# Sparse attention and gated MLP on one Trainium2 core: another way into the first batch's attention

## The chip, the cores and the metric

One core of a Trainium2 chip runs the whole program. The metric is device time in microseconds (us) of one execution. TensorE, VectorE, ScalarE, GpSimd and SyncE are written PE, DVE, ACT, POOL and SP, as in the profile. SP issues nearly all DMAs of this kernel, on one queue.

## The reference, cut to what matters

For 4 batches, 8 heads, 768 tokens and head size 64, each query sees the keys less than 16 tokens away and 24 summary keys, one per block of 32 tokens (the maximum over the block; the summary value is the mean). The result, 3072 rows of 512, goes through a gated MLP: `(x @ w_a * (x @ w_b)) @ w_out` with an inner size of 1536. The weights come as 64-bit floats, 18.9 MB, and are turned into pairs of 32-bit words (a high and a low part) on the chip.

```
k_sum = k.reshape(B, H, nb, block, D).max(axis=3)
v_sum = v.reshape(B, H, nb, block, D).mean(axis=3)
scores_l = scale * q @ k.T   where |i - j| < 16, else -1e9
scores_s = scale * q @ k_sum.T + log(32)
a = softmax(concat(scores_l, scores_s));  x = a @ concat(v, v_sum)
out = (x @ w_a) * (x @ w_b) @ w_out
```

## The kernel before, in words

**Tiling.** Query tiles have 128 tokens of all 8 heads. Tiles 0 to 3 (chunks 0 and 1, two tiles each) form the head of the kernel, `first_attention` (line 860); tiles 4 and 5 are chunk 2; the other three batches come in chunks of three tiles. The MLP is cut into 12 slices f of 128 inner columns. An item (`item`, line 1083) is one slice for one chunk: `up` (line 1056, matmuls of line 1067) makes the two products with w_a and w_b, four short steps on ACT and DVE form their product and split it into two parts, and `down` (line 1147, matmuls of line 1154) adds to the output. Slices 0 to 2 and 11 run for chunk 0 and chunk 1 apart, slices 3 to 10 for both together.

**The head's steps.** Keys come as six loads of 128 tokens by 8 heads, one token of one head a packet of 256 B (`first_keys`, lines 485 to 530). PE turns each with four transposes (line 441), DVE takes the block maxima from PSUM (line 508), ACT writes the turned keys to `kT` (lines 500, 501). Queries of a tile come in the same way, are turned (line 441) and scaled by ACT (line 938). For each tile, `scores` (line 638) has PE put the mask into PSUM (line 650) and add the score products (line 663); DVE takes maxima (line 700), ACT the exponentials (lines 721 and 729), DVE the sums and reciprocals, POOL the normalization (line 755). `transposes` (line 761) turns the result (line 768) and ACT copies it (line 780); `values` (line 846, matmuls of line 816) multiplies by the value rows, which come in three loads a tile (`load_values`, line 624, packets of 256 B); ACT and DVE split the result into the x that the MLP reads (lines 835 and 839).

**Value means.** Three loads of 512 KB bring all values, 16 tokens of a head in a partition. Load 0 is summed over its tokens by one DVE reduction (line 899), loads 1 and 2 by four halving additions each on POOL (line 910). 20 small matmuls (line 921) join half blocks, ACT copies the result into the value buffers (line 957, twice) and POOL copies it on to the other tiles' buffers (line 964, six times).

**Weights.** A part (slice f, and a, b or o for the three matrices) is a 512 KB load (line 380), then `convert` (line 386): ACT line 405, DVE lines 408 and 416, ACT line 421 (the high part), POOL line 424 (the low part). A part is called W0a, W0b and so on below.

**Order.** Each operation is put on a list with what it reads and writes. `Work.emit` (line 94) then issues them. The table `ORDER` (line 24) holds, for each engine, the numbers of the operations in the order in which that engine has them for the first part of the program (up to slice 6 or so on PE); after it, a planner with cost estimates chooses. Every engine works strictly in its order. With the numbers resolved, the head before is:

- SP: the six key loads, q0, value load 0, q1, value loads 1 and 2, W0a, q2, W0b, W0o, one value-row load of tile 1, W1a, q3, the three value-row loads of tile 0, the other two of tile 1, W1b, W2a, ...
- PE: keys; turn q0, masks 0, scores 0; turn q1, masks 1, scores 1; transposes and means; turn q2, masks 2, scores 2; values 0; turn q3; values 1; masks 3, scores 3; a transpose of tile 2; then the first up (slice 0 of chunk 0).

Of the kernel before, what the change touches and what calls it, by code (L numbers as in the profile page):

```python
# [29 lines left out]
    ],  # L30
    "ACT": [
# [8 lines left out]
    ],  # L40
    "DVE": [
# [8 lines left out]
    ],  # L50
    "POOL": [
# [3 lines left out]
    ],  # L55
# [88 lines left out]
def attention_moe(  # L144
# [33 lines left out]
    MEANS = "DPP"  # L178
# [61 lines left out]
    pairs = sb([P, 96], "pairs")  # L240
    nc.gpsimd.memset(pairs, 1.0 / BLK)
    for base, sign in ((32, 1), (-31, -1)):
        nc.gpsimd.affine_select(
            out=pairs, in_=pairs, compare_op=ALU.is_ge, fill=0.0, base=base,
            pattern=[[-2 * sign, 96]], channel_multiplier=sign,
        )
# [1031 lines left out]
```

## Time and profile before

| what | us |
|---|---|
| median of 3 runs (lowest to highest) | 654.5 (653.66 to 655.36) |
| span of the profiled execution, first to last instruction | 652.4 |
| PE busy in that span | 639.0 |

The page gives the profiled execution's span; a whole time of that execution is not listed beside it. Between the span and the median lie 2.1 us (1.3 to 3.0 us against the lowest and the highest run). PE's granted clock is 0.997 of full speed on the mean of the span. The span is read in two stretches: the head up to the first item, and the long rest in which PE has one matmul behind the other.

### The profile page before, as it was taken

What the parts mean: (1) busy time and instruction counts of PE and PEld (TensorE: products, weight loads), DVE (VectorE), ACT (ScalarE), POOL (GpSimd) and SP (SyncE); (2) the same over time, 40 slices, a digit from 0 to 9 for tenths busy, and PEclk for the clock granted to TensorE, in tenths of its full rate; (3) what the DMA queues carried; (4) which work ended last, traced back from release to release, by engine and by line L of the source; (5) the groups of instructions that cost most, each with busy time, mean ns of one, the idle gap of its engine ahead of it and who ended that gap; (6) DMA issues with size and microseconds to landing.
All of it is one profiled execution on the core that took longest, in us unless ns stands there. A gap on an engine that the chain in (4) does not pass through costs nothing.

```text
span 652.4 us, 12782 instructions
## 1 busy us (share of the span) xinstructions
PE 639.0 (98%) x4911; PEld 591.7 (91%) x4911; DVE 398.0 (61%) x866; ACT 242.6 (37%) x694; POOL 155.8 (24%) x238
## 2 busy tenths in 40 slices
PE   7799999999999999999999999999999999999997
PEld 4598888899999999999999999999999999999996
DVE  5877899987887584676676763756766632122212
ACT  4886787324443231422334312343323321121111
POOL 6782667523223222123222100111001100000000
PEclk9899999999999999999999999999999999999999
DMA  9999993552422233513114230142110200010001
GB/s 242 277 284 267 296 240 72 102 125 56 104 63 82 50 72 64 128 39 81 33 34 119 54 56 12 26 102 40 32 25 1 72 1 0 2 49 0 1 1 48
DMA packets 153108, 54.68 MB, mean 84 GB/s; under 512 B 133192, under 2 KB 145736, under 8 KB 153048
## 3 DMA queue, kind: packets, MB, share of 16 engines
q1 hardware_dynamic: 152904, 53.75, 34.0%
q8 instruction: 38, 0.62, 0.4%
q14 instruction: 22, 0.18, 0.1%
q10 hardware_dynamic: 144, 0.13, 0.1%
HBM read 47.12 MB, written 6.29 MB: 82 GB/s over the span
## 4 chain that ended last, share of the span: by engine, by line
PE 90%; DMA 4%; SPq 2%; ACT 1%; POOL 1%; DVE 1%; issue 0%; DVEq 0%; POOLq 0%; ACTq 0%
PE h L1067 55%; PE o L1154 28%; DMA raw<-in_moe_w_b_dram 4%; PE c L663 3%; PE o L816 3%; SPq L342 2%; POOL w L424 1%; PE h L816 0%; ACT S L405 0%; DVE c L408 0%; PE c L816 0%; PE c L1067 0%; POOL space L755 0%; DVE S L416 0%; PE o L768 0%
## 5 line engine op out<-in xcount | busy, mean ns | idle before, releaser
L1067 PE MATMUL h<-x,w 128*128 128x384 f32 (+2 forms) x2100 | 390.5, 320 | 0.1
L1067 PEld LDWEIGHTS h<-x,w 128*128 128x128 f32 x2100 | 334.1, 190 | 9.5 <-DVE x L839 0.7
L1154 PE MATMUL o<-w,gh 128*128 128x512 f32 x731 | 175.2, 382 | 0.0
L1154 PEld LDWEIGHTS o<-w,gh 128*128 128x128 f32 x731 | 134.5, 189 | 18.0 <-issue 2.4
L1135 DVE TENSOR_TENSOR h<-h,g 128x384 f32<-128x384 f32 (+1 forms) x79 | 45.7, 579 | 134.7 <-PE h L1067 134.3
L1137 ACT CAST gh<-h 128x384 fp32r<-128x384 f32 x71 | 34.0, 480 | 220.8 <-DVE h L1135 216.4
L800 DVE STREAM_TRANSPOSE pt<-s 32x256 f32<-32x256 f32 x228 | 99.3, 436 | 11.6 <-POOL s L755 7.9
L755 POOL TENSOR_TENSOR s<-s,nml 128x480 f32<-128x480 f32 x44 | 43.5, 989 | 229.6 <-DVE nml L751 193.6
L1067 PE MATMUL h<-late,w 128*128 128x384 f32 x288 | 94.0, 326 | 0.0
L729 ACT ACTIVATE s<-s,nml 128x120 f32<-128x120 f32 x160 | 61.5, 387 | 35.1 <-DVE nml L700 35.1
L1132 ACT COPY g<-h 128x384 f32<-128x384 f32 (+1 forms) x80 | 39.2, 490 | 55.4 <-PE h L1067 54.5
L1067 PEld LDWEIGHTS h<-late,w 128*128 128x128 f32 x288 | 54.4, 189 | 1.2 <-DVE late L839 0.2
L1140 DVE TENSOR_TENSOR gh<-h,gh 128x384 fp32r<-128x384 f32 x71 | 39.5, 556 | 22.0 <-ACT gh L1137 21.3
L692 DVE SCALAR_TENSOR_TENSOR s<-c,mask 128x480 f32<-128x480 f32 x40 | 26.0, 652 | 26.7 <-PE c L663 26.4
L587 POOL TENSOR_TENSOR S<-S 96x256 f32<-96x256 f32 (+3 forms) x58 | 33.2, 572 | 35.4 <-DMA S<-in_v_dram 32.9
L1154 PE MATMUL o<-w,x 128*128 128x512 f32 (+1 forms) x133 | 32.6, 381 | 0.2 <-DVE x L1108 0.2
L424 POOL TENSOR_TENSOR w<-S,w 128x512 fp32r<-128x512 f32 x24 | 30.4, 1286 | 7.3 <-ACT w L421 6.9
L408 DVE TENSOR_SCALAR c<-raw 128x512 int32<-128x512 uint32 x36 | 28.4, 804 | 5.6 <-DMA raw<-in_moe_w_b_dram 3.0
L729 ACT ACTIVATION_READ_ACCUMULATOR s<-s,nml 128x1 f32 x160 | 30.3, 190 | 0.0
L1154 PEld LDWEIGHTS o<-w,x 128*128 128x128 f32 x133 | 24.4, 189 | 4.2 <-DVE x L1108 0.6
L700 DVE TENSOR_REDUCE nml<-s 128x4 f32<-128x480 f32 x40 | 25.8, 647 | 0.5
L405 ACT ACTIVATE S<-raw 128x512 f32<-128x512 f32 x24 | 20.4, 861 | 4.7 <-DMA raw<-in_moe_w_b_dram 4.3
(138 smaller groups left out, 446.3 us busy)
## 6 DMA issues: line engine op xcount, KB each, us to landing
raw<-in_moe_w_a_dram SPq DMA_DIRECT2D x12, 512.0 KB, 7.7
raw<-in_moe_w_b_dram SPq DMA_DIRECT2D x12, 512.0 KB, 8.6
raw<-in_moe_w_out_dram SPq DMA_DIRECT2D x12, 512.0 KB, 5.7
out_dram<-S SPq DMA_DIRECT2D x23, 256.0 KB, 2.1
S<-in_v_dram SPq DMA_DIRECT2D x24, 192.0 KB, 2.8
kin<-in_k_dram SPq DMA_DIRECT2D x38, 100.0 KB, 2.5
qin<-in_q_dram SPq DMA_DIRECT2D x112, 32.0 KB, 1.9
vw<-in_v_dram SPq DMA_DIRECT2D x17, 192.0 KB, 2.8
```

Of the source, the lines that this page charges most:

```text
L408: dve(rank, 0.66, [raw], [bk], lambda: nc.vector.tensor_scalar(out=z.bitcast(I32), in0=word(0).bitcast(U32), scalar1=2.0**-29, scalar2=7.0 ...
L424: lambda eng=nc.vector if near else nc.gpsimd: eng.tensor_tensor(out=half(1), in0=t, in1=half(0).bitcast(F32), op=ALU.subtract),
L587: lambda: nc.gpsimd.tensor_tensor(out=out, in0=i0, in1=i1, op=ALU.add),
L729: lambda h=h, c=c, more=more: nc.scalar.activation(y[h][:, c, :], x[h][:, c, :], AF.Exp, bias=m[:, 0, h, c : c + 1], scale=1.0, **more,),
L755: lambda h=h, r=r: nc.gpsimd.tensor_tensor(out=y[h], in0=y[h], in1=r[:, :, None].broadcast_to([P, NP, COLS]), op=ALU.mult,),
L800: lambda js=js, qs=qs, rs=rs: nc.vector.transpose(out=pv[js, rs, qs], in_=sv[qs, rs, js]),
L1067: nc.tensor.matmul(ps, w[:, c, part, :], xs[xpart][:, :, c].rearrange("p g (a b) -> p g b a", a=2), start=(i == 0), stop=(i == n - 1),)
L1132: act(CHAIN, 0.13 + W / 1030, ["h0"], gk, lambda: nc.scalar.copy(out=g, in_=pa))
L1135: lambda: nc.vector.tensor_tensor(out=pb, in0=pb, in1=g, op=ALU.mult),
L1137: act(CHAIN, 0.16 + W / 1030, [bk], ghks, lambda: nc.scalar.copy(out=gh, in_=pb))
L1140: lambda: nc.vector.tensor_tensor(out=gl, in0=pb, in1=gh.bitcast(F32), op=ALU.subtract),
L1154: nc.tensor.matmul(b, (gh if first else gl)[:, j * P : (j + 1) * P], y, start=(f == 0 or half is not None) and first and part == 0, stop=( ...
```

## The change

1. The keys of the first batch and the queries of tiles 0 to 3 are loaded two tokens to a partition: 512 B a packet, four heads and 256 tokens a load. Six key loads and four query loads stay (the first two key loads leave out 16 tokens, which come in a small load of their own). A query load now holds half the heads of two tiles, so tile 0 needs both q0 and q1, and tile 2 both q2 and q3.
2. Each load is turned by eight products with the unit matrix, 64 columns of the load as the stationary side, in the two column halves of PE in turn (`turn_twos`), in place of four transposes. DVE's maxima are then of 8 pairs of tokens, and three small maxima join them into blocks. ACT writes each turned key load in two copies (three for the first two).
3. The means: 24 products of the value loads with `pairs` on PE, one ACT copy (`vS`), eight products with `twin`. The reductions of lines 899 and 910 and the 20 matmuls of line 921 are gone.
4. The high parts of W0a, W0b, W0o and W1a are made by POOL (`ON_POOL`), no longer by ACT.
5. Six products of the unit matrix with itself (`warm`) stand first on PE.
6. `ORDER` is written anew and ends sooner (on PE with slice 3 of the joint items). Resolved:
   - SP: key load 4, the 16 tokens, key loads 0, 3, 1, 2, 5, q0, q1, W0b, value loads 0 to 2, q3, W1a, a value-row load of tile 0 (32 rows), q2, W0a, W0o, W1b, the other two of tile 0 (64 and 80 rows), the three of tile 1 (192 rows), W2a, ...
   - PE: warm; keys; turn q0, q1; masks and scores 0, masks and scores 1; the 24 products of the means; a transpose of tile 0, the eight `twin` products, the other transpose; turn q3, q2; masks 2, scores 2; transposes 1; values 0; masks 3; values 1; scores 3; then the first up.
   - ACT, from scores 1 on: exponentials of tile 0, of tile 1, `vS`, line 405 of W1a, copies of transposes, line 405 of W0a, scaling of q3 and q2, line 405 of W0o, mean copy 1, line 405 of W1b, mean copy 0, transposes 1, x of tile 0, exponentials of tile 2, x of tile 1.
   - POOL: high W0b, normalization 0, low W0b, high and low W1a, normalization 1, high W0a, two mean copies, high W0o, low W0a, ...

```
-    pairs = sb([P, 96], "pairs")
+    pairs, twin = sb([P, D], "pairs"), sb([P, D], "twin")
...
+    nc.gpsimd.tensor_tensor(out=twin, in0=ident[:, :D], in1=ident[:, D:], op=ALU.add)
...
+    ON_POOL = (0, 1, 2, 3)
...
+        if i in ON_POOL:
+            pool(rank - 0.5, 0.72, [key, raw], [hi], lambda: nc.gpsimd.tensor_copy(out=half(0), in_=t))
+        else:
+            act(rank - 0.5, 0.52, [key, raw], [hi], lambda: nc.scalar.copy(out=half(0), in_=t))
...
+    def turn_twos(bk, x):
+        for c in range(2):
+            for j in range(2):
+                for h in range(2):
+                    n, m = (2 * j + c) * P, (2 * c + h) * P + j * D
+                    nc.tensor.matmul(
+                        bank[bk][h * D : (h + 1) * D, n : n + P], x[:, m : m + D], ident,
+                        start=True, stop=True, tile_position=(0, h * D),
+                    )
...
-                i, 262.0, 208, (), [key], x.rearrange("p (h d) -> p h d", d=D),
-                heads(k[0, :, i * P : (i + 1) * P, :]),
+                i, 262.0, 280, (), [key], x[p0:].rearrange("p (h x) -> p h x", x=2 * D),
+                bass.AP(
+                    tensor=src.tensor, offset=src.offset + (256 * a - 16 + 2 * p0) * D,
+                    ap=[[2 * D, P - p0], [S * D, 4], [1, 2 * D]],
+                ),
...
+                nc.vector.tensor_reduce(
+                    out=hv[:, a, 2 * g : 2 * g + 2, :],
+                    in_=bank[bk].rearrange("p (j c n x) -> p c n j x", j=2, c=2, x=8),
+                    axis=AX.XY, op=ALU.max,
+                )
...
+    def warm():
+        for i in range(6):
+            nc.tensor.matmul(bank["o0"][:, :P], ident, ident, start=True, stop=True)
...
-            if MEANS[n] == "D":
...
+                    nc.tensor.matmul(
+                        bank["h1"][:, n * D : (n + 1) * D], x[:, i * P : (i + 1) * P], pairs,
+                        start=(i == 0), stop=(i == 7),
                     )
...
+        act(FIRST, 0.35, ["h1", "P26.1"], ["vS"], lambda: nc.scalar.copy(
+            out=vS, in_=bank["h1"][:, : H * NS]
+        ))
+        pe(FIRST + 0.5, 0.7, ["vS", "P26.1"], ["h0"], lambda: [
+            nc.tensor.matmul(
+                bank["h0"][WIN:COLS, h * D : (h + 1) * D], vS[:, h * NS : (h + 1) * NS], twin,
+                start=True, stop=True, tile_position=(0, WIN),
+            )
+            for h in range(H)
+        ])
...
-        begin(2, "o0")
+        ask(1, ("o0", "o1"))
+        begin(2)
```

## Rows read from the trace of the kernel before

**Rows 1.** Page: busy us, share of the span and instructions of each engine

```profile
PE 639.0 (98%) x4911; PEld 591.7 (91%) x4911; DVE 398.0 (61%) x866; ACT 242.6 (37%) x694; POOL 155.8 (24%) x238
```

**Rows 2.** Windows: stretch, length, busy PE/PEld/DVE/ACT/POOL, clock, DMA share, GB/s

```profile
0.00:33.90 33.90, 25.30 (x289) 18.42 (x289) 23.37 (x49) 22.23 (x55) 23.87 (x62) 0.95 1.03 264
33.90:65.40 31.50, 30.99 (x271) 28.44 (x269) 22.42 (x42) 22.90 (x56) 16.93 (x17) 1.00 1.04 272
65.40:640.00 574.60, 574.60 (x4311) 537.46 (x4310) 348.58 (x770) 194.37 (x579) 115.05 (x161) 1.00 0.27 63
```

**Rows 3.** Timeline of PE, head: start, length, line, operation, count, [idle before, releaser]

```profile
4.41 1.09 PE L441 MATMUL h<-ident,space 128*128 128x128 f32 x4 [4.41 <-POOL mask L229]
...
11.51 0.63 PE L441 MATMUL c<-ident,space 128*128 128x128 f32 x4
...
19.02 0.65 PE L768 MATMUL o<-ident,s 128*120 128x128 f32 x4 [2.49 <-POOL s L755]
19.61 0.51 PE L921 MATMUL h<-space,pairs 128*24 128x64 f32 x6
...
28.39 1.16 PE L816 MATMUL h<-pt,vw 120*64 120x64 f32 x32
...
30.06 1.34 PE L816 MATMUL h<-space,space 120*64 120x64 f32 x32
31.38 1.20 PE L650 MATMUL o<-space 128*128 128x512 f32 x4
...
33.49 0.65 PE L768 MATMUL o<-ident,s 128*120 128x128 f32 x4
33.90 2.92 PE L1067 MATMUL h<-x,w 128*128 128x256 f32 x24
```

**Rows 4.** Chain of waits, 0 to 70 us: start, length, what

```profile
11.67 10.58 DMA raw<-in_moe_w_b_dram
```

**Rows 5.** Timeline of ACT and DVE, head: columns as in rows 3

```profile
25.50 1.18 ACT L957 COPY vw<-h 24x512 f32<-24x512 f32 x2
...
26.17 0.70 DVE L408 TENSOR_SCALAR c<-raw 128x512 int32<-128x512 uint32 x1 [0.64 <-DMA raw<-in_moe_w_a_dram]
26.71 0.69 ACT L405 ACTIVATE space<-raw 128x512 f32<-128x512 f32 x1
...
27.31 0.60 ACT L421 CAST w<-S 128x512 fp32r<-128x512 f32 x1
...
31.72 0.60 ACT L835 CAST x<-h 128x512 fp32r<-128x512 f32 x1
...
32.90 0.66 DVE L839 TENSOR_TENSOR x<-h,x 128x512 fp32r<-128x512 f32 x1
```

**Rows 6.** DMA totals of 5 to 10, 19 to 21 and 25 to 28 us

```profile
DMA packets 4390, 1.11 MB, mean 222 GB/s; under 512 B 4389, under 2 KB 4389, under 8 KB 4390
...
DMA packets 435, 0.75 MB, mean 373 GB/s; under 512 B 73, under 2 KB 321, under 8 KB 434
...
DMA packets 1660, 0.41 MB, mean 138 GB/s; under 512 B 1660, under 2 KB 1660, under 8 KB 1660
```

**Rows 7.** Timeline of POOL and DVE, head: columns as in rows 3

```profile
6.71 0.29 POOL L317 CAST space<-ident 128x128 fp32r<-128x128 f32 x1
6.95 0.40 POOL L318 CAST space<-mask 128x256 fp32r<-128x256 f32 x1
...
12.79 1.95 DVE L899 TENSOR_REDUCE space<-space 128x64 f32<-128x1024 f32 x1 [0.36 <-DMA space<-in_v_dram]
...
15.42 2.60 POOL L910 TENSOR_TENSOR space<-space 128x512 f32<-128x512 f32 x2 [2.63 <-DMA space<-in_v_dram]
...
18.93 1.84 POOL L910 TENSOR_TENSOR space<-space 128x256 f32<-128x256 f32 x3
...
21.66 1.14 POOL L910 TENSOR_TENSOR space<-space 128x64 f32<-128x64 f32 x3
```

**Rows 8.** Windows, 21.8 to 25.1 us: columns as in rows 2

```profile
21.80:25.10 3.30, 3.30 (x20) 2.68 (x21) 2.33 (x6) 2.83 (x6) 0.93 (x3) 0.50 1.16 258
```

More of the change, by code (lines that the diff above doesn't have):

```diff
@@ L177, in attention_moe @@
     COPIES = ("AA", "AA", "AA", "AA")
-    MEANS = "DPP"
     TURNS = 5
@@ L322, in attention_moe @@
     mask_kind(2)
-    work = Work({"POOL": 10.9, "DVE": 2.3, "ACT": 2.3, "PE": 3.0, "SP": 0.8})
+    work = Work({"POOL": 10.9, "DVE": 2.3, "ACT": 2.3, "PE": 1.6, "SP": 0.8})
+    work.add("-", 0, 0, 8.3, (), MK, lambda: None)
     def pe(rank, takes, reads, writes, fn):
@@ L420, in convert @@
         )
-        act(rank - 0.5, 0.52, [key, raw], [hi], lambda: nc.scalar.copy(out=half(0), in_=t))
+        if i in ON_POOL:
+            pool(rank - 0.5, 0.72, [key, raw], [hi], lambda: nc.gpsimd.tensor_copy(out=half(0), in_=t))
+        else:
+            act(rank - 0.5, 0.52, [key, raw], [hi], lambda: nc.scalar.copy(out=half(0), in_=t))
         (dve if near else pool)(
@@ new lines, in twos @@
+    def twos(bk):
+        return bank[bk].rearrange("p (j c i y) -> p c i y j", j=2, c=2, i=2)
+    def first_keys():
+        hv = spaces["P26"][:, 512 : 512 + 4 * 48].rearrange("p (a c n) -> p a c n", a=3, c=4)
+        ends = spaces["P16"][:8].rearrange("p (h x) -> p h x", x=2 * D)
+        src = k[0]
+        load(
+            0.5, 33.0, 60, (), ["kx"], ends,
+            bass.AP(
+                tensor=src.tensor, offset=src.offset + (S - 16) * D,
+                ap=[[2 * D, 8], [S * D, H], [1, 2 * D]],
+            ),
+        )
+        for i in range(6):
+            a, g = i // 2, i % 2
+            x, key = area(16 + a)
+            x, key = x[:, g * 512 : (g + 1) * 512], key[g]
+            p0 = 8 if a == 0 else 0
+            src = k[0, 4 * g]
+            load(
+                i, 262.0, 280, (), [key], x[p0:].rearrange("p (h x) -> p h x", x=2 * D),
+                bass.AP(
+                    tensor=src.tensor, offset=src.offset + (256 * a - 16 + 2 * p0) * D,
+                    ap=[[2 * D, P - p0], [S * D, 4], [1, 2 * D]],
+                ),
@@ new lines, in put @@
+            def put(bk=bk, a=a, g=g):
+                cs, js = slice(2 * g, 2 * g + 2), slice(2 * a, 2 * a + 2)
+                x = "p c i (y j) -> p c i y j"
+                for out, ys in (
+                    (kper[:, cs, js, :WIN], slice(0, WIN // 2)),
+                    (kper[:, cs, js, COLS:], slice(WIN // 2, 64)),
+                ):
+                    nc.scalar.copy(
+                        out=out.rearrange(x, j=2), in_=twos(bk)[:, :, :, ys, :]
+                    )
+                if a == 0:
+                    nc.scalar.copy(
+                        out=kT[:, cs, KC - 32 : KC - 16].rearrange("p c (y j) -> p c y j", j=2),
+                        in_=twos(bk)[:, :, 0, :8, :],
+                    )
@@ new lines, in first_keys @@
+        for out, i0, i1 in (
+            (kv[:, :, :, :7], hc[:, :, :, 1:14:2], hc[:, :, :, 2:15:2]),
+            (kv[:, :, :2, 7], hc[:, :, :2, 15], hc[:, :, 1:, 0]),
+            (kv[:, :, 2, 7], hc[:, :, 2, 15], hc[:, :, 0, 0]),
+        ):
+            dve(
+                FIRST, 0.15, [f"ksi{i}" for i in range(6)] + ["P26.1"], ["ksall"],
+                lambda out=out, i0=i0, i1=i1: nc.vector.tensor_tensor(
+                    out=out, in0=i0, in1=i1, op=ALU.max
+                ),
+            )
@@ L527, in first_keys @@
         for c in range(NP):
-            work.add("-", 0, 0, 0, [f"ksi{i}" for i in range(6)], [f"ks{c}"], lambda: None)
+            work.add("-", 0, 0, 0, ["ksall"], [f"ks{c}"], lambda: None)
             work.add("-", 0, 0, 0, KB, [f"kT{c}k"], lambda: None)
@@ L644, in scores @@
         masked = u < FILL
-        near = [f"kB{i}" for i in range(max(t - 1, 0), t + 2)] + [f"kBs{int(t > 1)}"]
+        near = [f"kB{i}" for i in range(t // 2 * 2, (t + 1) // 2 * 2 + 2)] + [f"kBs{int(t > 1)}"]
         def masks():
@@ L672, in scores @@
         if lead is None:
-            pe(-1, 1.06, [qk] + (near if masked else KT), banks, fn)
+            pe(-1, 1.06, qk + near if masked else [qk] + KT, banks, fn)
         else:
@@ L858, in attention_moe @@
     PD = (pbuf, [[x for x in PT if (x[2] in "01") == (h == 0)] for h in range(2)])
+    def warm():
+        for i in range(6):
+            nc.tensor.matmul(bank["o0"][:, :P], ident, ident, start=True, stop=True)
     def first_attention():
+        pe(-1, 2.5, (), ["o0"], warm)
         first_keys()
@@ L916, in means @@
-            def means(n=n):
-                for h in range(H):
-                    i = 2 * NS * h - n * P
-                    if not -2 * NS < i < P:
-                        continue
-                    nc.tensor.matmul(
-                        bank["h0"][WIN:COLS, h * D : (h + 1) * D],
-                        pairs[:, 16 + i // 2 : 16 + i // 2 + NS], rows[:, n, :],
-                        start=i >= 0, stop=i + 2 * NS <= P, tile_position=(0, WIN),
-                    )
-            pe(FIRST + 0.5, 0.4, [f"vr{n}"], ["h0"], means)
@@ new lines, in first_attention @@
+        act(FIRST, 0.35, ["h1", "P26.1"], ["vS"], lambda: nc.scalar.copy(
[5 more added lines that the diff above has]
+                start=True, stop=True, tile_position=(0, WIN),
+            )
+            for h in range(H)
+        ])
+        for g in range(4):
+            load_values(0, g, vws[g], vks[g][:3], (16, 18, 20.5, 20.7)[g])
@@ new lines, in ask @@
+        def ask(a, banks):
+            for i, bk in enumerate(banks):
+                x, key = queries[2 * a + i]
+                rank = rank_of(a)
+                pe(rank, 0.9, [key], [bk], lambda bk=bk, x=x: turn_twos(bk, x))
+                act(
+                    rank, 0.58, [bk], [f"q{i}"],
+                    lambda bk=bk, i=i: nc.scalar.mul(
+                        out=qT[:, :, 2 * i : 2 * i + 2].rearrange("p i c (y j) -> p c i y j", j=2),
+                        in_=twos(bk), mul=0.125,
+                    ),
+                )
```

101 lines of the change are left out of this document (39 added, 62 removed), and 48 rows, old and new, of the table ORDER.

## Prediction, made before the changed kernel was run

> **What bounds the kernel now.** I read the page first: PE is busy for 639.0 of 652.4 us [rows 1], so only PE's idle time and PE's work can shorten the span. The windows then say where the idle time lies. From 0 to 33.9 us PE is busy 25.30 of 33.90, from 33.9 to 65.4 it is busy 30.99 of 31.50, and from 65.4 to 640 it never stops [rows 2]. So 8.6 us stand idle in the head, 0.5 us in the stretch after it, and none in the long rest, which the change does not touch. The timeline of PE shows what the head's gaps are: 4.41 us before the first key is turned, 2.49 us before the first transpose of tile 0, and some smaller ones; the first up starts at 33.90, after the last transpose that began at 33.49 [rows 3]. From there PE's order holds the same work in both kernels. **The whole question is when the first up can start, and whether PE stays fed afterwards.**
>
> The chain of waits says what the head hangs on: a weight load, issued at 11.67 and 10.58 us long [rows 4]. The DMA share stands at 1.03 through the head [rows 2], so the queue of loads hardly rests. A later landing on the same queue is W1a, for which DVE waited until 26.17 [rows 5]. I use it as the anchor, since in both kernels nearly the same loads stand ahead of this place.
>
> **The price of a 512-byte packet.** No load here has such packets. From 5 to 10 us all packets but one are of 256 B and the queue moves 222 GB/s; from 19 to 21 us, with mostly larger ones (1 KB for W0a and W0b), it moves 373 GB/s [rows 6]. A 262 KB load takes 1.18 us at the first rate and 0.70 us at the second; those are the bounds, and a gain below nothing is left out, since a packet of 512 B is at worst two of 256 B. Per packet on one of 16 DMA engines that is 18.5 ns for 256 B and 43.9 ns for 1 KB, and a line between them gives 27 ns for 512 B: 303 GB/s, 0.86 us a load, 0.32 us saved on each of ten. I take that; a cost per packet with a cost per byte fits both rows.
>
> The Trainium skill says otherwise (DMA: Bandwidth & Descriptors, Specifications): transfers reach line rate from 512 B on, and the fabric's ceiling is 435 GB/s. By that a load would take an estimated 0.60 us. The rows neither reach that rate nor hold such packets; this is the first rival below.
>
> **Where the queue stands when the first up needs it.** Ahead of W1b stand in the new order all that stood ahead of W1a, and q3, W1b and the 16 tokens (32 KB, 0.1 us) besides; one value-row load of 32 rows stands there in both. So W1b lands at 26.17 - 9 x 0.32 + 0.86 + 0.1 + 1.41 (512 KB at 373 GB/s) = 25.7 us. Behind it come two value-row loads of tile 0, 144 rows of 2 KB, and three of tile 1, 192 rows: at 222 GB/s 1.33 and 1.77 us. They land at 27.0 and 28.8 us. The worse bound is the stretch from 25 to 28 us, where the packets are all small and only 138 GB/s flow [rows 6]: 5.0 us for both, 1.9 us more.
>
> ACT works in order and has line 405 of W1b and then the second mean copy ahead of the transposes of tile 1 and of x: 25.7 + 0.69 + 0.59 (1.18 for two) [rows 5] = 27.0 us, the same time as the value rows of tile 0. What waits behind that in ACT's queue is due later than the rows anyway.
>
> **From there to the first up.** Values 0 take 1.16, masks 3 1.20, values 1 1.34 us [rows 3], each with some 0.1 us under the next: 27.0, 28.1, 29.2, 30.4. ACT's part of x, 0.60, and DVE's, 0.66 [rows 5], end at 31.7. Scores 3 run meanwhile. So the first up starts at 31.7 instead of 33.9, 2.2 us earlier. The transpose of tile 2 that ended just ahead of it before comes after it now: 33.90 - 33.49 = 0.4 us [rows 3] are only moved. **Gain: 1.8 us.**
>
> **What costs nothing, and its cover.**
> - Turning by products: a load takes eight products of 64 stationary and 128 moving columns. 32 value products with 64 moving columns take 1.16 us [rows 3], 36 ns each, so eight of twice the length take 0.58 us, against 0.63 us for four transposes at the upper clock level. The early four at 1.09 us [rows 3] ran at the lower level by their length. About 1.1 us a load there is more than the 0.86 us of a load, so at the lower level PE would lag by 0.2 us a load and cover is thin: with six keys up to 1.4 us, all in a part that has 3 us of slack before the value rows.
> - The means on PE: 24 products and eight. Six of the old means took 0.51 us [rows 3], 85 ns each, so 32 take 2.7 us; by the loading of a whole 128-column load at the pace of a transpose (0.63 / 4) up to 4.5 us. They lie behind scores 1, where PE had 2.49 us idle [rows 3] and now waits for the exponentials. Without that cover it would be 0.5 to 2.5 us after the 20 old ones are taken off.
> - DVE loses 1.95 us, and POOL loses 2.60 + 1.84 + 1.14 us of additions, eight in all [rows 7]. DVE gains three small maxima. POOL gains four casts: 0.29 us for 128 columns and 0.40 for 256 [rows 7] make 0.62 for 512, 2.5 us in all, so POOL ends 3.1 us to the good. ACT loses four casts of 0.60 [rows 5] and gains one short copy.
> - POOL's new first cast waits for W0b and holds the normalization of tile 0 behind it. W0b lands some 2 us before the exponentials of tile 0 are done, so that wait is covered; PE and the transposes are who would wait.
> - Line 405 of W0a on ACT holds the scaling of q3 and q2 behind it, and so masks 2 and scores 2. It costs PE idle time at 21 to 24 us, covered by the value rows, which come later still.
> - The six warm products lie in PE's first 4.41 idle us [rows 3].
> - SP issues the same number of loads and one small one more; each queue moves only in its order, which is counted above.
>
> **Sum.** 652.4 us of span less 1.8 is 650.6; the profiled execution has no time of its own shown, and the median stands 2.1 us above its span, so 654.5 - 1.8 = **652.7 us**. A measurement of this kernel tells about 0.3% from no change, 2.0 us: the forecast lies just inside that.
>
> **Rival 1, packets of 512 B at full rate (faster).** At 373 GB/s a load takes 0.70 us and W1b lands at 26.17 - 9 x 0.48 + 0.70 + 0.1 + 1.41 = 24.1 us; everything behind it follows 1.6 us earlier, the first up at 30.1: a gain of 3.4 us, 651.1 us. For it: from 512 B the skill's page (above) promises line rate, by which the estimate would come out 1 us lower still. Against it: the queue also holds unequal loads, and ACT's and PE's own work then begins to bind. Chance 0.24.
>
> **Rival 2, the clock takes it back (no change).** After the idle 2.49 us and the gaps behind it PE's granted clock stood at 0.50, the lower level of 1.2 GHz, from 21.8 to 25.1 us [rows 8]. In the new order PE idles from about 21 to 24 us, behind ACT's wait for W0a. If the clock then falls and is still low at 28 to 30 us, values 0, masks 3 and values 1 stretch by up to 1.4 us on the path: gain 0.4 us, 654.1 us. For it: the same kind of gap did it before. Against: the fall would have to last into the value products. Chance 0.14.
>
> **Rival 3, the value rows of tile 1 land last and late (slower).** They now stand behind W1b. If 512 B packets flow no faster than 256 B ones (the change then does not do what it says) and the value rows flow at 138 GB/s, W1b lands at 26.17 + 1.18 + 0.1 + 1.41 = 28.9, the rows at 33.9, the first up at 33.9 + 1.3 + 0.6 + 0.7 = 36.4, which is 2.9 us lost with the moved transpose: 657.4 us. The fault decides once the rows land after 31.0 us. With the slow rows alone they land at 30.7 (654.2 us), with the slow packets alone at 32.0 (655.5 us). For it: the stretch of 138 GB/s is there. Against: it came as these loads were issued with little else queued, and W0a, W0o and W1b now stand ahead of them. Chance 0.14.
>
> **How the numbers follow.** The forecast has 0.48; its own range, 651.8 to 653.6, comes from 1 us of slip in the queue either way, and nearly half of it lies beyond 2.0 us of gain. Faster: 0.24 and 0.22 of the forecast, 0.46. Slower: the worse part of rival 3 and 0.03 for waits later on (PE's hand order ends sooner, with slice 3): 0.14. The same: 0.40. The range reaches from 650.3, rival 1 with a little more, to 655.6, rival 3 with slow packets alone.
>
> **What the profile after would show.** The key loads landing about 0.9 us apart instead of 1.2; PE's products of the means between scores 1 and the transposes; ACT waiting for W0a and W1b; the first up near 31.7 us; PE without gaps from there on. I am wrong if the first up starts early and PE idles later (before, 0.5 us from 33.9 to 65.4 and none to 640), if values 1 wait for something other than their rows, or if the clock stays at the lower level through the scores.

## The result, and the profile after

The changed kernel takes **658.98 us** (median of 4 runs, 657.73 to 659.8) against 654.08 (4 runs, 653.56 to 655.36): a ratio of 1.0075, 95% interval 1.0059 to 1.0091. It is 4.9 us slower. The forecast was 652.7 in a range up to 655.6, so direction and range were both wrong.

The windows of the changed kernel, the first two over the stretches of [rows 2], then on to 150 us (columns as there):

```profile
0.00:33.90 33.90, 30.80 (x432) 26.58 (x436) 21.48 (x46) 19.70 (x53) 21.52 (x60) 1.00 1.03 267
33.90:65.40 31.50, 30.84 (x300) 28.89 (x299) 27.48 (x55) 27.47 (x63) 20.19 (x18) 1.00 0.97 247
65.40:100.00 34.60, 32.80 (x175) 27.19 (x174) 30.70 (x46) 28.05 (x51) 23.53 (x19) 1.00 1.04 285
100.00:150.00 50.00, 49.97 (x410) 44.13 (x409) 40.83 (x99) 17.99 (x60) 23.24 (x33) 1.00 0.44 94
```

Two things stand out. In the head PE is busy for 30.80 us, 5.5 us more than the 25.30 before: it has been given work. And from 65.4 to 100 us, where it never stopped before, it idles for 1.8 us. The timeline shows what PE's busy head is (start, length, line, operation, count, idle before):

```profile
1.43 2.93 PE L913 MATMUL o<-ident 128*128 128x128 f32 x12 [1.43 <-POOL ident masks.py:199]
4.36 1.09 PE L490 MATMUL h<-ident,space 128*64 128x128 f32 x16
6.12 1.09 PE L490 MATMUL c<-ident,space 128*64 128x128 f32 x16 [0.66 <-DMA space<-in_k_dram]
7.02 1.07 PE L490 MATMUL o<-ident,space 128*64 128x128 f32 x16
8.39 1.09 PE L490 MATMUL c<-ident,space 128*64 128x128 f32 x16 [0.30 <-DMA space<-in_k_dram]
9.31 1.04 PE L490 MATMUL o<-ident,space 128*64 128x128 f32 x16
10.19 1.04 PE L490 MATMUL h<-ident,space 128*64 128x128 f32 x16
11.06 1.92 PE L490 MATMUL c<-ident,space 128*64 128x128 f32 x32
12.90 1.20 PE L701 MATMUL o<-space 128*128 128x512 f32 x4
14.03 1.05 PE L714 MATMUL o<-kT,space 64*64 64x120 f32 x32
...
17.12 5.57 PE L959 MATMUL h<-pairs,space 128*128 128x64 f32 x48
22.53 0.60 PE L819 MATMUL o<-ident,s 128*120 128x128 f32 x4
23.10 1.07 PE L970 MATMUL h<-twin,space 128*24 128x64 f32 x16
24.10 0.65 PE L819 MATMUL o<-ident,s 128*120 128x128 f32 x4
24.68 1.97 PE L490 MATMUL o<-ident,space 128*64 128x128 f32 x32
27.35 1.20 PE L701 MATMUL o<-space 128*128 128x512 f32 x4 [0.70 <-ACT space L986]
...
30.48 1.15 PE L867 MATMUL h<-pt,vw 120*64 120x64 f32 x32
...
32.68 1.15 PE L867 MATMUL h<-space,space 120*64 120x64 f32 x32
33.76 1.05 PE L714 MATMUL o<-kT,space 64*64 64x120 f32 x32
35.24 2.94 PE L1122 MATMUL h<-x,w 128*128 128x256 f32 x24 [0.43 <-DVE x L890]
```

From 9.31 to 35.24 us PE waits for 1.1 us in all. The first up starts at 35.24 instead of 33.90 [rows 3]. The sums of the three value loads (line 959) alone take 5.4 us (17.12 to 22.53). Earlier PE waits twice for key loads, 0.66 and 0.30 us. Neither value product waits for its rows. The normalizations of tile 0 are done before PE gets to the transposes: on POOL they run from 19.05 to 20.98, and ACT then stands idle behind the sums. POOL's and ACT's timeline:

```profile
19.05 1.93 POOL L806 TENSOR_TENSOR s<-s,nml 128x480 f32<-128x480 f32 x2 [0.90 <-DVE nml L802]
...
22.73 0.32 ACT L966 COPY space<-h 128x192 f32<-128x192 f32 x1 [2.92 <-PE h L959]
```

The idle time later is at two places of PE's timeline, both waits for x, which ACT writes at line 1192 (before: line 1137):

```profile
73.44 2.00 PE L1209 MATMUL o<-w,x 128*128 128x512 f32 x8 [0.46 <-ACT x L1192]
82.75 1.99 PE L1209 MATMUL o<-w,x 128*128 128x512 f32 x8 [1.27 <-ACT x L1192]
```

So two suspects: the head, where the first up comes 1.34 us later, and what follows 65 us, where the table `ORDER` no longer reaches.

### The profile page after: what moved, and what is told of

Its sections match the earlier page's. It is cut to its first block, busy times and chain, and to the rows that moved or that the text cites. A ratio compares the mean times of both kernels' runs of the same rounds, so it can differ in the third digit from the quotient of the medians.

```text
span 657.1 us, 13157 instructions
## 1 busy us (share of the span) xinstructions
PE 647.1 (98%) x5087; PEld 601.0 (91%) x5087; DVE 399.8 (61%) x868; ACT 240.7 (37%) x693; POOL 153.1 (23%) x235
## 4 chain that ended last, share of the span: by engine, by line
PE 85%; DMA 5%; SPq 5%; DVE 2%; ACT 1%; issue 1%; DVEq 0%; ACTq 0%
PE h L1122 51%; PE o L1209 27%; PE o L867 3%; PE c L714 3%; SPq L338 3%; SPq L377 2%; DMA raw<-in_moe_w_out_dram 1%; DMA S<-in_k_dram 1%; DMA raw<-in_moe_w_a_dram 1%; DMA space<-in_k_dram 1%; ACT w L421 1%; DVE c L405 0%; DMA kin<-in_k_dram 0%; PE c L867 0%; PE c L1122 0%
## 5 line engine op out<-in xcount | busy, mean ns | idle before, releaser
L867 PEld LDWEIGHTS o<-pt,vw 120*64 120x64 f32 x576 | 18.3, 138 | 4.3 <-issue 3.6
```

Of the source, the lines that this page charges most:

```text
L867: nc.tensor.matmul(ps[h * D : (h + 1) * D, c, es], vw[e][:COLS, 2 * c + h, :], d[:COLS, h, c, es], start=True, stop=True, tile_position=(0 ...
```

## The experiments

Times are medians; each ratio is to the kernel before, timed in the same batch (653.4 to 653.95 us), with its 95% interval. "First up" is its start in the one profile of each run; it is 33.90 before and 35.24 after. full_keys, small_load and loads_120 were executed once each and compute another result, as their expectations say; they are read for the queue and for PE's timeline, not for the time.

| run | built on | us | ratio (interval) | first up |
|---|---|---|---|---|
| long_order | after | 655.38 | 1.0020 (1.0011 to 1.0029) | 35.27 |
| short_order | before | 660.12 | 1.0092 (1.0079 to 1.0106) | 34.26 |
| late_means | after | 667.67 | 1.0209 (1.0195 to 1.0223) | 46.56 |
| means_back | long_order | 660.07 | 1.0100 (1.0085 to 1.0114) | 39.70 |
| products | before | 653.49 | 0.9994 (0.9985 to 1.0003) | 34.15 |
| loads_only | before | 655.95 | 1.0038 (1.0025 to 1.0051) | 36.94 |
| no_warm | long_order | 656.0 | 1.0037 (1.0024 to 1.0050) | 36.58 |
| full_keys | long_order | 654.12 | single run | 34.48 |
| unshifted | long_order | 654.8 | 1.0012 (1.0003 to 1.0021) | 35.38 |
| small_load | long_order | 655.09 | single run | 35.34 |
| loads_120 | long_order | 654.73 | single run | 35.11 |
| half_sums | unshifted | 653.71 | 0.9998 (0.9986 to 1.0011) | 32.45 |
| more_products | half_sums | 653.68 | 1.0001 (0.9992 to 1.0010) | 32.98 |
| late_turned | half_sums | 653.55 | 1.0006 (0.9996 to 1.0017) | 32.16 |
| best_order | late_turned | 656.74 | 1.0054 (1.0040 to 1.0068) | 33.87 |
| last_order | best_order | 658.22 | 1.0064 (1.0051 to 1.0078) | 33.54 |
| sums_only | before | 658.31 | 1.0071 (1.0058 to 1.0083) | 37.01 |
| sums_order | sums_only | 659.25 | 1.0081 (1.0068 to 1.0094) | 36.54 |

### The hand order's end, both ways

long_order gives the changed kernel the rest of the old table; short_order cuts the old kernel's table where the new one ends. The table holds numbers; here they are put in words.

```diff
 # long_order: ORDER["PE"] of the changed kernel (the other engines likewise)
-    ..., up A slice 3, up B slice 3
+    ..., up A slice 3, up B slice 3, downs slice 2, ups slice 4, scores 4, ..., down slice 6
```

> The changed kernel, with its hand order carried on by the order that the kernel before has from slice 3 on. If the 1.8 us of idle PE between 65 and 100 us come from the order that ends sooner, they go, and the time falls to 656.5 to 657.5. If they come from weights that are late, the idle time and 659 us stay.

> The kernel before, with its hand order cut where that of the changed kernel ends (PE after the second up of slice 3, the others about there). If the sooner end of the order costs time by itself, PE idles 1 to 2 us between 65 and 100 us and the time rises from 654.1 to 655 to 656. If not, it stays within 0.5 us of 654.1.

Long_order brought 3.6 us back (658.98 to 655.38); PE is busy for 34.60 of 34.60 us from 65.4 to 100, and the first up stays at 35.27:

```profile
65.40:100.00 34.60, 34.60 (x189) 30.00 (x188) 24.17 (x40) 22.14 (x47) 17.41 (x15) 1.00 0.98 274
```

Short_order lost 6 us with the head's order as before. Both came out larger than expected. Short_order's windows, and its longest wait from 60 to 110 us (releaser: total us, times, longest):

```profile
65.40:100.00 34.60, 32.89 (x179) 28.07 (x178) 31.70 (x48) 28.65 (x55) 23.00 (x20) 1.00 0.94 251
100.00:150.00 50.00, 48.55 (x379) 42.53 (x379) 45.36 (x102) 20.05 (x59) 21.54 (x28) 1.00 0.45 100
...
PE o L1146 <- ACT x L1129: 2.4, 2, 1.7
```

It is the same wait for x as in the changed kernel, at other times. Behind the table's end the planner puts weights ahead of the x that PE needs. In the changed kernel DVE's timeline shows it ahead of PE's wait at 82.75 (lines 405 and 413 are words of weights, line 1190 is the product that ACT's x comes from):

```profile
79.06 0.85 DVE L405 TENSOR_SCALAR c<-raw 128x512 int32<-128x512 uint32 x1
80.01 0.69 DVE L413 SCALAR_TENSOR_TENSOR S<-S,c 128x512 int32<-128x512 int32 x1
80.62 0.87 DVE L405 TENSOR_SCALAR c<-raw 128x512 int32<-128x512 uint32 x1
81.35 0.73 DVE L1190 TENSOR_TENSOR h<-h,g 128x512 f32<-128x512 f32 x1
```

DVE does words of weights and nothing else from 75.48 until then. **So 3.6 of the 4.9 us are the table's shorter end**, and none of them belongs to the loads, the products or the sums. The waits alone are less than that. From the first up to PE's last product the changed kernel's profile takes 617.5 us and that of long_order 613.7; 2.2 of these 3.8 us are PE's idle time, and in the rest PE is longer busy with the same products. Why it is longer busy was not traced.

### The sums on TensorE

late_means keeps the changed kernel and moves the sums behind tile 0's transposes on PE (and the copy behind them on ACT), so that the transposes do not wait for them.

```diff
 # late_means: order of PE, in words
-    scores 1, sums 0, sums 1, sums 2, tr 0.1, twin, tr 0.0, turn q3, ...
+    scores 1, tr 0.1, tr 0.0, sums 0, sums 1, sums 2, twin, turn q3, ...
```

> The changed kernel with the 24 products of the value sums and the eight that follow moved behind both transposes of tile 0 on PE, and the copy behind them moved on ACT; nothing else. If the sums, 5.6 us in front of transposes that are ready at 20 to 21 us, are what makes the first up late, the transposes come 1.5 to 2.5 us sooner, the first up starts at 33 to 34 instead of 35.2 us, and the time falls from 659.0 to some 657. If the landings of the loads set the first up, it stays within 0.5 us of 35.2 and the time of 659.

A clear miss, 8.7 us slower than the changed kernel, although the transposes start 2.2 us sooner (20.29 instead of 22.53). PE's timeline, and the window of the head:

```profile
20.29 2.05 PE L815 MATMUL o<-ident,s 128*120 128x128 f32 x8 [2.91 <-POOL s L802]
22.14 10.34 PE L955 MATMUL h<-pairs,space 128*128 128x64 f32 x48
...
0.00:33.90 33.90, 28.93 (x278) 26.29 (x279) 14.84 (x33) 13.60 (x41) 15.63 (x51) 0.80 1.00 269
```

PE now idles for 2.91 us ahead of the transposes, its granted clock falls (0.50, the lower of its two levels, from 22 to 33 us; 0.80 on the mean of the first 33.9 us), and the same 24 products take 10.34 us instead of 5.57. The cover that the prediction gave to the sums, the 2.49 idle us of [rows 3], is real, and with the sums in it the clock stays up (1.00 in the changed kernel); but the sums are twice as long as the hole.

means_back takes the sums off PE again and leaves the rest of long_order.

```diff
 # means_back, in words
-    24 products with pairs, copy vS, 8 products with twin   # PE, ACT
+    one DVE reduction, eight POOL additions, 10 products    # lines 899, 910, 921 of before
```

> The changed kernel with the long hand order, and the value sums made as before (one reduction on DVE, eight additions on POOL, 20 records on PE), with their places and those of the four casts on POOL set anew by hand; loads, unit products, warm products and casts as changed. If PE's 5.5 us of sums hold the head up, as PE is busy from 12.9 us to the first up but for some 1 us, the first up starts 2 to 4 us before 35.3 and the time is 651.5 to 653.5, under both kernels. If the loads or POOL bind in their place, the first up stays at 34 to 35.5 and the time at 654 to 656. A fall of PE's clock in the gap that the sums had filled would take 1 to 2 us back.

Another miss: 6.7 us above the kernel before, where long_order is 1.4 above it. PE idles for 6.00 us before the first transpose, and POOL, which normalizes ahead of it, waits for DVE:

```profile
22.91 1.11 PE L822 MATMUL o<-ident,s 128*120 128x128 f32 x4 [6.00 <-POOL s L809]
...
21.87 1.93 POOL L809 TENSOR_TENSOR s<-s,nml 128x480 f32<-128x480 f32 x2 [1.27 <-DVE nml L805]
```

In the order that I wrote, DVE's reduction of a value load stands ahead of the maxima of tile 0. It starts at 15.74, when its load has landed; so the maxima come at 17.58 instead of 15.15, ACT's exponentials at 18.25 instead of 15.84, and DVE's reciprocals follow. POOL's first additions are done by then. The run shows what that order costs; it does not price the sums.

half_sums prices them. POOL adds the two halves of each value load, so that PE has 12 products left.

```diff
+    pool: x[:, :512] = x[:, :512] + x[:, 512:]
-    for i in range(8): matmul(h1, x[:, i * P : (i + 1) * P], pairs, stop=(i == 7))
+    for i in range(4): matmul(h1, x[:, i * P : (i + 1) * P], pairs, stop=(i == 3))
```

> The kernel of the run with unshifted keys, with the value sums halved on POOL ahead of PE (one addition of 512 columns a load, 12 products on PE instead of 24), POOL's order of the head set anew. If PE's work in the head sets the first up, it comes 2 to 2.7 us before that of the run with unshifted keys, and the time is 651 to 652.5, under both kernels. If the value rows' landing or POOL bind, it comes less than 1 us sooner and the time is 653 to 654.5.

The first up comes at 32.45, 2.9 us before that of unshifted (explained below), from which it differs in the halving and POOL's order alone, and 1.45 before that of the old kernel. Scores 0 and the first up in unshifted, then in half_sums, and the first up in more_products (the next run):

```profile
14.15 1.05 PE L690 MATMUL o<-kT,space 64*64 64x120 f32 x32
35.38 2.94 PE L1098 MATMUL h<-x,w 128*128 128x256 f32 x24 [0.43 <-DVE x L866]
...
13.09 1.05 PE L690 MATMUL o<-kT,space 64*64 64x120 f32 x32
32.45 2.94 PE L1104 MATMUL h<-x,w 128*128 128x256 f32 x24 [0.42 <-DVE x L866]
...
32.98 2.94 PE L1105 MATMUL h<-x,w 128*128 128x256 f32 x24 [0.43 <-DVE x L866]
```

Not all of the 2.9 us are the sums: 1.06 us stand already at scores 0, where PE turned the first keys faster in this profile, and 1.9 come behind it. In more_products, whose scores 0 start at 14.11 as in unshifted, the halving gives 2.4 us. So the sums hold the head, as expected; half of them is worth some 2 us there. But the time fell by only 1.1 us, to 653.71, no different from before. PE's last product ends 2.6 us sooner than in unshifted; 1.6 of them are lost after it. The DMA view of half_sums, the last microseconds (issue: count, KB, us to landing; the instruction fetch is that of 648 to 649 us):

```profile
q8 instruction: 1, 0.02, 5.8%
...
out_dram<-S SPq DMA_DIRECT2D x1, 128.0 KB, 4.1
```

The last store lands 4.1 us after its issue, 2.5 in the kernel before and in unshifted, and an instruction fetch lies in it. (This profiled execution took 654.17 us, the second longest of eleven; whether the others have the late store is not known.) more_products moves that fetch by giving PE 24 more records and no more time ahead of the keys:

```diff
-        for i in range(6):
-            nc.tensor.matmul(bank["o0"][:, :P], ident, ident, start=True, stop=True)
+        for i in range(18):
+            m = P if i < 4 else 8
+            nc.tensor.matmul(bank["o0"][:m, :m], ident[:, :m], ident[:, :m], start=True, stop=True)
```

> half_sums with the six unit products ahead of the first keys made four of 128 columns and fourteen of 8, so that TensorE has some 24 records more and the stage ahead of the keys is as long. If the lost 1.5 us of half_sums are the instruction fetch beside the last store, the fetch moves ahead of 645 us, the last store lands 2.5 us after its issue instead of 4.1, and the time is 652.2 +- 0.5. Rival: the store is late for another reason and the time stays within 0.5 of half_sums's 653.7.

The same view of more_products (the fetch in its window of 638 to 640 us):

```profile
q8 instruction: 1, 0.02, 2.9%
...
out_dram<-S SPq DMA_DIRECT2D x1, 128.0 KB, 2.5
```

The store lands in 2.5 us with the fetch out of its way, as it does in unshifted, which has as many PE records (5087; half_sums 5063) and its fetch at 641 us. So in these profiles the late landing goes with the fetch beside it. The time did not fall: scores 1 start at 16.22 instead of 15.20, PE ends 0.95 us later (647.55 against 646.60), so the span fell by 0.6 us alone and the median not at all. In this profile PE turns the first two key loads slowly (1.98 and 1.83 us), but so it does in unshifted, which has the six large products (1.98 and 1.80; scores 1 at 16.25); that the small products cost this time is not shown.

### The loads of two tokens and their products

products is the old kernel with its transposes replaced; loads_only is the old kernel with the new loads and their products, everything else as it was, in the old order.

```diff
 # products, in turn (line 435 of before)
-            nc.tensor.transpose(dst[:, c * P : (c + 1) * P], src[:, c * P : (c + 1) * P], ident)
+            for h in range(2):
+                n = c * P + h * D
+                nc.tensor.matmul(dst[h * D : (h + 1) * D, c * P : (c + 1) * P], src[:, n : n + D], ident,
+                                 start=True, stop=True, tile_position=(0, h * D))
```

> The kernel before, with the four transposes of each load of keys and queries replaced by eight products with the unit matrix in the two column halves; loads, order and the rest as before. If these products take twice what the transposes take (16 records where I counted eight), the keys are turned at 1.9 us a load at the lower clock level and 1.0 at the upper one, scores 0 start 1 to 4 us after 13.0, and the time rises by 1 to 4 us. If they take what I forecast (0.58 us a load), the time stays within 0.5 us of 654.1.

> The kernel before with the two-token loads and the unit products alone (means and casts as before, no warm products, the order of before with the loads of q1 and q3 and their turns moved ahead, as the new layout asks). My forecast gave these loads 0.32 us each: then the later landings come 1 to 3 us sooner and the time falls by 0.5 to 2 us under 654. If the head is bound by PE, ACT and POOL from 12 us on and not by landings, the time stays within 0.7 us of 654. If the wait for two query loads before scores 0 costs, it rises by 0.5 to 1.5 us.

products changes nothing that can be measured (653.49). Its key turns take 1.98 and 1.05 us, about twice what I had forecast, as the expectation's first branch had it; but the head before has PE idle, and scores 0 start only 0.6 us later (13.62 instead of 12.99). loads_only is 2.5 us slower: the new loads do not bring the keys sooner, scores 0 start at 15.50. Of the 1.9 us behind products, 0.9 are the second query load that PE must turn first (1.93 us for two, 1.05 for one). no_warm takes the six products off long_order:

```diff
-        pe(-1, 2.5, (), ["o0"], warm)
```

> The changed kernel with the long hand order and without the six warm products. If they are what puts PE on the upper clock level before the first keys, the unit products of the first keys take 2.0 us a load instead of 1.0, scores 0 start 1 to 4 us after 14.0, and the time rises by 1 to 4 us over 655.4. If the clock rises anyway by then, nothing changes by more than 0.5 us.

It starts the first up 1.3 us later than long_order, and its ratio is 0.0017 higher, 1.1 us, with intervals that overlap: the key products then take 1.97 us a load until about 9.4 us, against 1.49 for the first and 1.09 from then on. So the six products do quicken the keys; that the time gains by it is likely and not clear of noise. I call the slow pace the lower clock level because it is half the other one, as the clock's fall in late_means halves the pace of the sums. The granted clock of these profiles does not show it: its mean reads 1.00 from 4 to 10 us in no_warm too.

Why the loads were no faster is the work of four runs. unshifted loads the keys from token 0 on and writes them to other columns, so that every load has 128 partitions and the small one is gone. full_keys has the same loads with the writes left as they were, small_load keeps only the small load, loads_120 only the loads of 120 partitions.

```diff
-            p0 = 8 if a == 0 else 0
+            p0 = 0                                      # full_keys, unshifted, small_load
...
-        load(0.5, 33.0, 60, (), ["kx"], ends, ...)      # 8 partitions; full_keys, unshifted, loads_120
```

> The changed kernel with the long hand order, all six key loads with 128 partitions and without the small load of 16 tokens (so the keys stand 16 tokens off their places in the products, and the result is another one). If loads of 120 and of 8 partitions are what keeps the queue at 215 to 236 GB/s from 3 to 8 us, it moves 280 GB/s or more there, and the last key load is turned 0.5 to 1 us sooner than 10.2. If packets of 512 B are no faster among other packets of 512 B at that place, the rate stays at 215 to 240.

> The changed kernel with the long hand order and keys loaded without the shift by 16 tokens: six loads of 128 partitions, no small load, no third ACT copy, maxima taken over whole blocks of 32 tokens (so the three small maxima go). The result is the same as the reference's. If the loads of 120 and 8 partitions are what is left of the loss, the queue moves 280 GB/s or more from 3 to 8 us, scores 0 start 1.0 to 1.5 us before 14.0, the first up at 33.8 to 34.4, and the time is 653.5 to 654.5, that of the kernel before. If PE's sums alone set the first up, it stays at 35.2 and 655.4.

> The changed kernel with the long hand order, all key loads with 128 partitions, and the small load of 8 partitions kept but put where nothing reads it (the keys then stand 16 tokens off their places). If the small load by itself holds the queue, it moves 215 to 240 GB/s from 3 to 8 us as in the changed kernel; if the loads of 120 partitions do, it moves 275 or more.

> The changed kernel with the long hand order, two key loads of 120 partitions as in the change, and no small load (its eight partitions are zeros, so 16 keys are left out). If the loads of 120 partitions hold the queue, it moves 215 to 240 GB/s from 3 to 8 us and load k1 is turned at 8.2 us or later; if the small load does, 275 or more and 7.7.

The windows from 3 to 8 us (last number GB/s) of the kernel before, with its packets of 256 B, then of long_order, which has both irregular loads,

```profile
3.00:8.00 5.00, 3.41 (x13) 2.27 (x14) 0.69 (x1) 1.37 (x5) 4.26 (x19) 1.00 1.27 230
...
3.00:8.00 5.00, 4.57 (x53) 3.93 (x54) 0.69 (x1) 0.60 (x1) 4.28 (x20) 1.00 1.02 229
```

and of full_keys, which has neither:

```profile
3.00:8.00 5.00, 5.00 (x63) 4.78 (x63) 0.82 (x2) 0.95 (x1) 4.28 (x20) 1.00 1.07 293
```

unshifted has 286, small_load 264, loads_120 250. So packets of 512 B flow at 286 to 293 GB/s when each load has 128 partitions, near the 303 that the prediction took, and at 227 to 229, no faster than the 230 of the kernel before, once the 16 tokens are split off; either irregular load alone takes part of it, which is neither branch of the expectations of small_load and loads_120. But little comes of it: against the kernel before in their own batches, unshifted stands 0.85 us above, long_order 1.4 (and the one execution of full_keys 0.8). And the first ups of full_keys and unshifted lie 0.9 us apart with the same loads. In unshifted PE turns the first two key loads at the pace of the lower clock level (1.98 and 1.80 us), in full_keys only the first (1.79). When the pace rises differs between such profiles, and that is worth as much as the loads are. With regular loads PE's products, not the loads, set the keys' pace: eight products every 0.87 us, without a wait. In the changed kernel its two waits for key loads, 0.96 us together, come on top.

### Looking for a version that beats both

late_turned gives half_sums the old loads and transposes for tiles 2 and 3; best_order and last_order then change the order alone. sums_only is the old kernel with the halved sums and the order that they need; sums_order is sums_only with its order rewritten. In the expectations the "prelu" of a weight is ACT's line 405, its "word" DVE's lines 408 and 416, and the "epsilons" are small additions of DVE ahead of the reciprocals.

```diff
 # late_turned, cut
-        ask(1, ("o0", "o1"))               # 16 products, two loads of 512-byte packets
+        for g in (2, 3): pe(... turn(bank["h1"], x)); act(... qT[:, g % G] ...)
 # sums_only, on before, in words
-    reductions and additions of lines 899 and 910, 10 products of line 921
+    half sums on POOL, 12 products with pairs, vS, 8 with twin; masks 3 ahead of values 1
```

> half_sums with the queries of tiles 2 and 3 loaded one token per partition and turned by four transposes each, as before, and turned into a bank that is free earlier. TensorE saves 2 x (1.0 - 0.6) us between the first sums and scores 2. If TensorE still binds there, masks 2 starts at 22.5 to 23 instead of 24.2 and the first up at 31.3 to 31.8 instead of 32.45; TensorE has 24 records fewer, so that the late instruction fetch should not come, and the time is 651.8 to 652.5. Rival: value rows or W bind instead, the first up stays at 32.2 to 33 and the time at 652.5 to 653.7.

> The kernel before with one part of the change alone: the value sums on TensorE, from halves that GpSimd adds, with masks 3 ahead of values 1; loads, transposes and casts as before, no products ahead of the keys. If the loads of two tokens and their products bring nothing, scores 0 stays at 13.0, the sums end near 19.5, the first up comes at 31.5 to 32.2 instead of 33.9 and the time is 652.0 +- 0.6, under that of half_sums. Rival: the two-token loads carry the gain of half_sums; here W1b and the value rows land some 2.5 us later, the first up stays at 33.3 to 34.2 and the time at 653.4 to 654.4.

> late_turned with another order alone: copies of the means ahead of the prelu of W0a and W0o, W0o loaded behind the value rows of tiles 0 and 1, normalizations of tile 2 ahead of the low part of W1b, exponentials of tile 3 ahead of the prelus of W2a and W1o. If order held late_turned back, values 0 starts near 26 instead of 27.3, the first up at 30.5 to 31.2 instead of 32.16, no wait of 0.73 before the transposes of tile 2, and the time is 651.5 to 652.5, under both kernels. Rival: value rows or weights land too late or ACT binds: first up 31.5 to 32.3, time 652.8 to 653.7.

> sums_only with another order of DVE, ACT and GpSimd behind the sums (epsilons and reciprocals ahead of the words of weights, W1a and the value rows ahead of W0o). If order held sums_only back, the normalizations of tile 1 come near 23.5 instead of 30, the first up at 31.5 to 33 instead of 37.0 and the time is 652.5 to 654. Rival: with 256-byte packets everything behind lands some 2.5 us later and the weights bind: first up 34 or later, time 654.5 or more.

> best_order with another order alone: the low part of tile 1 right behind the sums of tile 2, the word of W0o loaded ahead of the value rows of tile 1 and combined later, values 2 ahead of the transposes of tile 3. If order alone held best_order back, the first up comes at 30.5 to 31.5 instead of 33.87 with no fall of the granted clock, and the time is 651.3 to 652.7, under both kernels. Rival: the weights of the second up or the exponentials of tile 3 then bind and PE gives the gain back between 31 and 50 us: time 653 to 655.5.

late_turned brings masks 2 from 24.17 to 22.16, but values 0 then wait 1.52 us for mean copies, which stand on ACT behind a step of W0o that waited for its load until 25.35; 653.55, no gain. The other four missed. In best_order values 1 end 1.1 us sooner than in late_turned, and the first up waits 3.36 us for x, which stands on DVE behind the words of W0o, the first of which waited for its load until 28.39, and behind sums of a tile. last_order puts that right, and the loads are next:

```profile
26.22 1.16 PE L843 MATMUL h<-pt,vw 120*64 120x64 f32 x32 [0.76 <-DMA vw<-in_v_dram]
27.31 1.19 PE L677 MATMUL o<-space 128*128 128x512 f32 x4
30.82 1.16 PE L843 MATMUL h<-space,space 120*64 120x64 f32 x32 [2.31 <-DMA space<-in_v_dram]
```

Here the value rows bind, as the prediction had it for the change itself, and from 40 to 46 us PE is busy for 3.32 us, before for 5.86. sums_only and sums_order are held by waits in the orders that I wrote (1.23 and 1.41 us ahead of the transposes of tile 0 or the twin products, 1.40 and 2.61 us for x), and do not say what the halved sums alone are worth. No run is faster than the kernel before; half_sums, more_products, late_turned and products equal it.

## Why the prediction was wrong

- **"0.03 for waits later on (PE's hand order ends sooner, with slice 3)".** This step failed most. I saw the shorter table, gave it a chance of 0.03 and no price, and wrote that the change does not touch the long rest. It cost 3.6 us in the changed kernel and 6 us in the old one.
- **"eight of twice the length take 0.58 us".** I took 32 records of line 816 for 32 products; the code has 16. Each product of 32-bit floats leaves two records (line 959: 24 products, 48 records), so the price a product was half the true one. Eight products take 0.87 to 1.05 us at the upper level, against 0.63 for four transposes. The same slip is in the old means: the "20 small matmuls" of line 921 are 10 products with 20 records.
- **"so 32 take 2.7 us; ... up to 4.5 us", covered by 2.49 idle us.** The sums take 5.4 us and the twin products 1.0. The transposes could have started at 20.0 to 20.3 (the first normalization is done at about 20.0; in late_means they start at 20.29); they started at 22.53. That is 2.2 to 2.5 us on the path, and halving the sums gave 1.9 to 2.4 back. Taking the cover from the idle time before was right in kind (late_means); its size was not held against the upper bound that I had written down. Together with the unit products this is the head's whole miss: values 0 start at 30.48 instead of 27.0, and PE runs up to there from 17.12 with one wait of 0.70 us. From values 0 to the first up it takes 4.8 us, forecast 4.7.
- **"0.32 us saved on each of ten".** Nothing was saved: 227 GB/s from 3 to 8 us. The rate for 512 B was about right for regular loads (286 to 293), and the loads of 120 and 8 partitions undid it; I had counted the small one as 0.1 us and the others as full. My 303 took the packets of the 373 GB/s row for 1 KB. The row has 435 packets for 0.75 MB, 1.7 KB each; with that the same line gives an estimated 291 GB/s. The Trainium skill's rule (DMA: Bandwidth & Descriptors, Specifications) that transfers reach line rate from 512 B on does not show here: by it these loads would have come at an estimated 435 GB/s, and the best row with such packets has 293.
- **"Where the queue stands when the first up needs it."** The chain through W1b and the value rows did not bind: neither value product waits for rows in the changed kernel. PE's own work filled the head before the loads could. In last_order, where PE is ahead, they do bind.
- **What held.** The early products lie in PE's idle 4.4 us, and the keys behind them are turned faster (no_warm is 1.1 us slower than long_order by the ratios, with intervals that overlap). The granted clock of 0.50 at 21.8 to 25.1 us [rows 8] is gone, it is 1.00 over the first 33.9 us, so rival 2 did not come. The casts on POOL made no wait on PE in the head; they were never undone alone, so that they cost nothing is argued, not shown.
- **Rival 3** had the sign and nearly the size (657.4), but that is luck. Its condition on the packets did come (227 GB/s against 230 for those of 256 B); the late value rows that were to cost the time did not hold PE up.

The sum as it was: some 1.3 us from the first up, 3.6 from the table's end, together the 4.9 measured. Long_order's remaining 1.4 us over the kernel before fit its first up at 35.27 instead of 33.90. That an earlier first up is worth as much is not shown: half_sums has it 1.45 us before the old kernel and the same time.

## What to carry to other kernels

When a table of hand order is rewritten, the place where it ends is part of the change: cut or extend it by itself in a run before pricing anything else. Count the products in the code and the records in the profile for the same line before you divide a busy time by a count. Work moved into an engine's idle hole is free only up to the hole's length; once that engine is full, its own time is the path, and faster loads gain nothing until it is relieved.

## What the runs showed of the hardware that was not expected

- A product of 32-bit floats shows as two records: 24 products as 48, at some 225 ns a product with 128 stationary and 64 moving columns.
- Loads of 120 or 8 partitions among loads of 128 came with a slower queue, in one profile each: 286 and 293 GB/s without them, 264 with the load of 8, 250 with those of 120, 227 and 229 with both.
- 2.91 idle us of PE were followed by the lower clock level (granted clock 0.50 from 22 to 33 us): 24 products took 10.34 us instead of 5.57.
- With one 16-KB instruction fetch beside it the last store landed in 4.1 us instead of 2.5. With 24 PE records more the fetch came at 639.6 us (more_products) and 641 (unshifted) instead of 648 to 649.
